# Adding two products in PSUM for the last four groups of a fused attention and rational-activation kernel, with the whole issue order written anew

## The chip, the cores and the metric

The kernel runs on one core of one Trainium2 chip. The metric is the device time of one execution in microseconds (us), lower is better. The core has five engines with in-order queues that run side by side: TensorE (PE in the profile, with its weight loads as PEld), VectorE (DVE), ScalarE (ACT), GpSimd (POOL) and SyncE (SP); sixteen DMA engines move data for all of them.

## The reference

Four batches, four heads, 1088 tokens and head dimension 32. Each head's queries and keys are turned into 64 features, the products of two projections; linear attention with these features gives `num / den`. The four heads side by side give 4352 tokens of 128 channels, and these go through one block with a rational activation:

```
phi(x)  = outer(S1 x, S2 x)                     # 8 x 8 = 64 features
x       = (phi(q) @ (phi(k)^T v)) / (phi(q) . sum phi(k) + 1e-6)
h       = x @ w_in                              # 128 -> 2048
P       = a0 + a1 h + a2 h^2 + a3 h^3
Q       = 1 + |b0| |h| + |b1| h^2
out     = (P / (Q + 1e-6)) @ w_out              # 2048 -> 128
```

The arrays are drawn from a fixed seed, and everything that comes in or goes out is float32.

## The kernel before, in words

The tokens are cut into ten chunks n: chunk 0 has 128 tokens, chunk 1 has 384, chunks 2 to 8 have 512 each, and chunk 9, the last, has 256 (64 left over from each batch). For each chunk the attention part (`add_keys`, `add_queries`) makes `xT`, 128 channels by the chunk's tokens. The 2048 hidden channels are 16 blocks of 128; a group g is one chunk with some of these blocks, laid side by side in the free dimension. There are 23 groups: 0 to 2 for chunk 0, 3 and 4 for chunk 1, two per chunk up to 18, and 19 to 22 for the last chunk, with 8, 4, 3 and 1 blocks (2048, 1024, 768 and 256 columns; `LAST`, line 159). A full group has 4096 columns.

`add_group` (from line 784) is one group. Its steps, by the names in the code:
- `h g,s`: TensorE multiplies by `w_in` in float32 into an `h_ps` tile of 1024 columns in PSUM. There are two such tiles, so `h` waits until the one before the last is emptied.
- `hev g,s`: the tile is cast to bf16 into `hb`. ScalarE does it; for the pieces in `CASTS` (line 161) VectorE does.
- `abs g` and `sq g`, VectorE: |h| into `u` (line 850) and h^2 into `lin` (line 858). The inputs are scaled at the start so that Q is 1 + kappa(|h| + h^2).
- `+Q g`: `u += lin`. With "Q" in the group's entry of `PLANS` (line 160) it is a DMA with an adding write that POOL issues (line 924), otherwise an addition on VectorE (line 920).
- `ln g` and `exp g`, ScalarE: ln(1 + kappa u) into `L` (line 872), and exp(-L), which is 1/Q, into `u` (line 875).
- `odd g`, `oddt g`, VectorE: the odd part of P into `y` (lines 862 and 868). `even g` (line 865) and `+P g` add the even part; `+P` goes by DMA with "P" in the plan.
- `n5 g`, VectorE: `y` times 1/Q (line 868).
- `py g`: TensorE multiplies `y` by the scaled `w_out` into `out_ps`. With "z" in the plan the constant a0 doesn't go through P: instead `pr g` multiplies `u` by a0 `w_out` into the same `out_ps`.
- `oev`, `otr`, `otev` and the store, per chunk: `out_ps` is copied by ScalarE, transposed by TensorE, copied again by ScalarE and stored by SP. They are numbered one less than the chunk: `oev 6` belongs to groups 15 and 16, `oev 7` to 17 and 18; for the last chunk there is only `otev 8`.
- `hot i`: a few bf16 matmuls of 512 columns on zeros into a spare tile, nothing uses them; `HOT` (line 164) gives their number.

The order of all this is not found when the kernel runs, nor by a scheduler: `Plan` collects the steps, and `ORDER` (line 19) is a written-out list of their numbers. `issue` emits them in this order, and each engine gets its own steps in this order. A step that has to wait holds up everything behind it on its engine. The costs and due times that stand in the `plan.add` calls are used only where there is no `ORDER`. The weights `w_out` are loaded by SP into a `y` tile; VectorE (`w0 0`, `w0 1`, line 436) and ScalarE (`w1 0`, `w1 1`, line 435) scale them once.

```
                nc.gpsimd.dma_start(out=dst(), in_=src(), accum_op=AX.add, max_dma_last_dim=GW)
...
        dq = add_up("+Q", u, sq, [ab, sp], g - 0.5)
        dq0 = dq if dq["engine"] == "DVE" else dq["after"][0]
        e = plan.add("ACT", gw * 0.846 + 170, ln, after=[dq, c_a] + got("L"), rank=g - 0.4, take=take("L"), name=f"ln {g}")
        e = used(plan.add("ACT", gw * 0.835 + 102, ex, after=[e], rank=g - 0.4, give=give("L"), name=f"exp {g}"), "L")
```

Of the kernel before, what the change touches and what calls it, by code (L numbers as in the profile page):

```python
# [16 lines left out]
PSUM = bass.MemoryType.PSUM  # L17

ORDER = [
# [36 lines left out]


class Plan:
# [66 lines left out]
def kernel(  # L125
# [31 lines left out]
    HEAD = 1  # L157
    FIRST = [4, 4, 8]
    LAST = [8, 4, 3, 1]
    PLANS = {**{g: "QP" for g in range(4, 20)}, **{g:"QPz" for g in range(13,20)},5:"QP",3:"Q",4:"sQP",17:"Qz",19:"QPz",20:"z",21:"z",22:"z"}  # L160
    CASTS = {18:(6,),16:(6,),14:(6,),12:(6,),17:(6,),13:(6,),15:(6,),11:(6,),10:(6,),8:(6,),9:(6,)}
    PACKED = (0, 9)
    BY_TOKEN = (9,)
    HOT = [6, 2, 5, 5, 6, 11, 4, 4, 6]
# [82 lines left out]
    def load(eng, fn, kb, n=1, rank=0.0, take=(), after=()):  # L247
        ring = landed[len(landed) + n - 9:][:1] if len(landed) + n > 8 else []
        i = plan.add(eng, (480 if eng == "SP" else 700) * n, lambda: fn(eng), after=list(after) + [last_of.get(eng)] + ring,
                     rank=rank, take=take, name="load")  # L250
        last_of[eng] = i
        if eng == "ACT":
            i = plan.add(eng, 1, lambda: None, after=[i], rank=rank, lag=1300, name="load")
        last_of["DMA"] = plan.add("DMA", kb * 1024 / 275, lambda: None, after=[i, last_of.get("DMA")], rank=rank,
                                  name="land")
        landed.extend([last_of["DMA"]] * n)
        return last_of["DMA"]
# [28 lines left out]
    ld["q", 0, 1] = load("SP", lambda e: load_main(e, "q_sb", q, 0, 1), 256, rank=-94)  # L286
    second = dict(mains(1))
    ld["wo"] = load("SP", load_wo, 800, rank=-93, take=["y"])
    ld["k", 1] = load("SP", second["k"], 512, 1, rank=-91, take=["kq"])
    ld["v", 1] = load("SP", second["v"], 512, NP, rank=-90, take=["v_aug"])  # L290
    ld["q", 1] = load("SP", second["q"], 512, 1, rank=-89, take=["kq"])
# [9 lines left out]

    zero = nc.const_aps.tensor(0.0, (128, 1), FP).bitcast(BF)[:, 0:1]
    ident = consts.tile([128, 128], FP, name="ident")
    mask4 = consts.tile([128, H], FP, name="mask4")
    mask12 = consts.tile([128, H, JC - HEAD], FP, name="mask12")
    mask2 = consts.tile([128, 2], FP, name="mask2")
# [80 lines left out]

    c_s12 = plan.add("DVE", 430, s_spread, after=[ld["s"], c_mask], rank=-98)
    c_s2 = plan.add("POOL", 250, s_expanded, after=[ld["s"], c_pool], rank=-3)
    c_m12 = plan.add("POOL", 100, pool_mask12, after=[c_pool], rank=-98.9, name="mask12")  # L390
    c_sw = {}
    for b in range(2):
# [391 lines left out]
    def add_group(g, G):  # L784
# [30 lines left out]
        def got(kind):  # L815
            return [T[kind, "got", n]] if packed else []
# [101 lines left out]
        def add_up(name, dst, src, after, rank, give=()):  # L918
            if name[1] not in how:
                return plan.add("DVE", tt, lambda: nc.vector.tensor_add(out=dst(), in0=dst(), in1=src()), after=after,  # L920
                                rank=rank, give=give, name=f"{name} {g}")

            def f():
                nc.gpsimd.dma_start(out=dst(), in_=src(), accum_op=AX.add, max_dma_last_dim=GW)  # L924
            p = plan.add("POOL", 1900, f, after=after, rank=rank, name=f"{name} {g}")
            return plan.add("DMA", -(-gw // 2048) * 2048 * 1.43 if gw > 1024 else gw * 1.43, lambda: None, after=[p], rank=rank, give=give, lag=900, name=f"{name} land {g}")
# [3 lines left out]
            sp = plan.add("ACT", gw * 0.835 + 102, square, after=hes + got("sq"), rank=g - 0.5, take=take("sq"), name=f"sq {g}")  # L930
        else:
            sp = plan.add("DVE", tt, square, after=hes + got("sq"), rank=g - 0.5, take=take("sq"), name=f"sq {g}")
        dq = add_up("+Q", u, sq, [ab, sp], g - 0.5)
        dq0 = dq if dq["engine"] == "DVE" else dq["after"][0]
        e = plan.add("ACT", gw * 0.846 + 170, ln, after=[dq, c_a] + got("L"), rank=g - 0.4, take=take("L"), name=f"ln {g}")
        e = used(plan.add("ACT", gw * 0.835 + 102, ex, after=[e], rank=g - 0.4, give=give("L"), name=f"exp {g}"), "L")
        p = plan.add("DVE", ts + 121, odd, after=[sp, c_a] + got("y"), rank=g - 0.3, take=take("y"), name=f"odd {g}")
        p = used(plan.add("DVE", tt, mul(y, y, ht), after=[p, ab], rank=g - 0.3, give=give("t"), name=f"oddt {g}"), "t")
# [146 lines left out]
```

## Time and profile before

| what | value |
|---|---|
| time, median of 3 runs (lowest to highest) | 246.72 us (246.26 to 246.79) |
| the profiled execution | 247.33 us |
| its span, first to last instruction | 245.3 us |
| busy: PE, DVE, ACT, POOL | 239.0, 223.5, 219.8, 48.4 us |

The profile is of one execution. The span leaves out 2.03 us around it. [...] Square brackets give the idle time before an instruction and who ended it.

### The profile page before, as it was taken

What the parts mean: (1) busy time and instruction counts of PE and PEld (TensorE: products, weight loads), DVE (VectorE), ACT (ScalarE), POOL (GpSimd) and SP (SyncE); (2) the same over time, 40 slices, a digit from 0 to 9 for tenths busy, and PEclk for the clock granted to TensorE, in tenths of its full rate; (3) what the DMA queues carried; (4) which work ended last, traced back from release to release, by engine and by line L of the source; (5) the groups of instructions that cost most, each with busy time, mean ns of one, the idle gap of its engine ahead of it and who ended that gap; (6) DMA issues with size and microseconds to landing.
All of it is one profiled execution on the core that took longest, in us unless ns stands there. A gap on an engine that the chain in (4) does not pass through costs nothing.

```text
span 245.3 us, 3066 instructions
## 1 busy us (share of the span) xinstructions
PE 239.0 (97%) x1148; PEld 138.4 (56%) x1148; DVE 223.5 (91%) x242; ACT 219.8 (90%) x199; POOL 48.4 (20%) x70
## 2 busy tenths in 40 slices
PE   8998999999999999999999999999999999999986
PEld 4887667665556486456464554435444444755453
DVE  0747889999999999999999999999999999999792
ACT  3237799898979998899999999999999999999993
POOL 7800021010121503011112111231311112111100
PEclk9999999999999999999999999999999999999999
DMA  6897706855869999999799999999999999999822
GB/s 159 266 319 178 259 12 123 165 169 97 150 117 184 174 191 222 212 196 179 128 181 180 184 175 176 229 170 187 184 187 191 212 191 172 193 194 188 158 88 64
DMA packets 22206, 42.96 MB, mean 175 GB/s; under 512 B 5536, under 2 KB 12720, under 8 KB 22064
## 3 DMA queue, kind: packets, MB, share of 16 engines
q0 software_dynamic: 8544, 31.74, 72.6%
q1 hardware_dynamic: 13360, 10.95, 14.6%
q8 instruction: 9, 0.15, 0.2%
q10 hardware_dynamic: 288, 0.08, 0.2%
q14 instruction: 5, 0.04, 0.0%
HBM read 8.82 MB, written 2.23 MB: 45 GB/s over the span
## 4 chain that ended last, share of the span: by engine, by line
PE 60%; ACT 35%; issue 3%; DVE 0%; ACTq 0%
PE h_ps L831 31%; ACT u L875 13%; ACT L L872 12%; PE w_ps L498 7%; ACT hb L838 6%; PE out_ps L888 4%; PE w_ps L463 3%; PE w_ps L627 3%; PE w_ps L685 2%; PE w_ps L673 2%; PE w_ps L617 2%; PE w_ps L454 1%; PE out_ps L359 1%; ACT q_pT L679 1%; ACT o_sb L893 1%
## 5 line engine op out<-in xcount | busy, mean ns | idle before, releaser
L831 PE MATMUL h_ps<-xT,w_in_sb 128*128 128x512 f32 (+3 forms) x320 | 126.3, 533 | 0.0
L831 PEld LDWEIGHTS h_ps<-xT,w_in_sb 128*128 128x128 f32 x320 | 55.5, 190 | 41.9 <-issue 31.9
L872 ACT ACTIVATE L<-u,kappa 128x4096 f32<-128x4096 bf16 (+6 forms) x23 | 66.2, 2884 | 0.1
L875 ACT ACTIVATE u<-L 128x4096 bf16<-128x4096 f32 (+6 forms) x23 | 64.3, 2801 | 0.1
L838 ACT CAST hb<-h_ps 128x1024 bf16<-128x1024 f32 (+3 forms) x53 | 54.5, 1051 | 4.8 <-PE h_ps L831 4.6
L924 POOL DMA_DIRECT2D u<-lin x17 | 20.8, 1224 | 120.4 <-DVE lin L858 29.0
L868 DVE TENSOR_TENSOR y<-y,u 128x4096 bf16<-128x4096 bf16 (+6 forms) x23 | 39.7, 1727 | 1.7 <-ACT u L875 1.6
L868 DVE TENSOR_TENSOR y<-y,hb 128x4096 bf16<-128x4096 bf16 (+6 forms) x23 | 39.5, 1725 | 0.0
L858 DVE TENSOR_TENSOR lin<-hb 128x4096 bf16<-128x4096 bf16 (+6 forms) x22 | 37.9, 1724 | 1.4 <-ACT hb L838 1.3
L888 PE MATMUL out_ps<-y,w_out_b 128*128 128x512 bf16 (+2 forms) x144 | 30.6, 355 | 0.2 <-DVE y L868 0.2
L924 POOL DMA_DIRECT2D y<-lin x15 | 19.0, 1268 | 59.5 <-DVE lin L865 27.0
L862 DVE TENSOR_SCALAR y<-lin,a_t 128x4096 bf16<-128x4096 bf16 (+6 forms) x23 | 24.6, 1068 | 0.3 <-ACT lin L856 0.2
L850 DVE TENSOR_SCALAR u<-hb 128x4096 int16<-128x4096 int16 (+6 forms) x23 | 21.6, 941 | 2.1 <-ACT hb L840 1.2
L888 PEld LDWEIGHTS <-w_out_b 128*128 128x128 bf16 x144 | 13.5, 98 | 16.0 <-issue 4.2
L498 PEld LDWEIGHTS w_ps<-v_aug,k_p 128*128 128x128 f32 x128 | 14.9, 192 | 1.4 <-ACT ab L470 0.8
L498 PE MATMUL w_ps<-v_aug,k_p 128*128 128x96 f32 x128 | 15.6, 276 | 0.0
L838 DVE CAST hb<-h_ps 128x1024 bf16<-128x1024 f32 x11 | 13.4, 1220 | 0.7 <-PE h_ps L831 0.7
L865 DVE TENSOR_SCALAR lin<-lin,a_t 128x4096 bf16<-128x4096 bf16 (+3 forms) x13 | 13.4, 1030 | 0.0
L673 PEld LDWEIGHTS w_ps<-ident,q_p 128*128 128x128 f32 x66 | 7.8, 141 | 7.5 <-issue 3.9
L1049 PE MATMUL w_ps<-const-float32-0.0 128*128 128x512 bf16 x49 | 11.8, 381 | 0.0
L679 ACT COPY q_pT<-w_ps 128x512 f32<-128x512 f32 (+2 forms) x18 | 10.9, 603 | 1.0 <-PE w_ps L673 1.0
L888 PE MATMUL out_ps<-u,w_out 128*128 128x512 bf16 x48 | 11.3, 379 | 0.0
(118 smaller groups left out, 226.6 us busy)
## 6 DMA issues: line engine op xcount, KB each, us to landing
u<-lin POOLq DMA_DIRECT2D x14, 1024.0 KB, 8.6
y<-lin POOLq DMA_DIRECT2D x13, 1024.0 KB, 9.5
v_aug<-in_v_dram SPq DMA_DIRECT2D x8, 256.0 KB, 4.9
out_dram<-oT SPq DMA_DIRECT2D x7, 256.0 KB, 7.5
kq<-in_k_dram SPq DMA_DIRECT2D x3, 512.0 KB, 4.7
kq<-in_q_dram SPq DMA_DIRECT2D x3, 512.0 KB, 7.7
u<-lin POOLq DMA_DIRECT2D x2, 768.0 KB, 7.0
w_in_sb<-in_moe_w_in_dram SPq DMA_DIRECT2D x1, 1024.0 KB, 6.6
```

The lines of the kernel that those rows point to most:

```text
L498: nc.tensor.matmul(kv_of((hp,))[:, 0], lhsT=lhs(hp), rhs=rhs(hp), start=(first and hp == hps[0]), stop=final, skip_group_check=True)
L831: nc.tensor.matmul(T["h", g, s][:, i * step:i * step + W], lhsT=w_in_sb[:, fi * 128:(fi + 1) * 128], rhs=T["xT", n][:, :W], start=True, st ...
L838: copy(out=T["t", g][:, s * W:(s + nsub) * W], in_=T["h", g, s][:, :nsub * W])
L850: nc.vector.tensor_scalar(out=u().bitcast(mybir.dt.int16), in0=ht().bitcast(mybir.dt.int16), scalar1=0x7FFF, scalar2=None, op0=AX.bitwise_and)
L858: nc.vector.tensor_mul(out=sq(), in0=ht(), in1=ht())
L862: nc.vector.tensor_scalar(out=y(), in0=sq(), scalar1=a_t[:, 3:4], scalar2=a_t[:, 1:2], op0=AX.mult, op1=AX.add)
L865: nc.vector.tensor_scalar(out=sq(), in0=sq(), scalar1=a_t[:, 0:1], scalar2=None, op0=AX.add)
L868: return lambda: nc.vector.tensor_mul(out=out(), in0=in0(), in1=in1())
L872: nc.scalar.activation(out=T["L", g][:, :gw], in_=u(), func=ACT.Ln, bias=1.0 + 1e-6, scale=kappa[:, 2:3])
L875: nc.scalar.activation(out=u(), in_=T["L", g][:, :gw], func=ACT.Exp, scale=-1.0)
L888: nc.tensor.matmul(T["o", n][:, :W], lhsT=w[:, fi, :], rhs=T[src, g][:, i * W:(i + 1) * W], start=(start and i == 0), stop=(stop and i == ...
L924: nc.gpsimd.dma_start(out=dst(), in_=src(), accum_op=AX.add, max_dma_last_dim=GW)
```

## The change

In groups 19 to 22 the sum |h| + h^2 isn't made in `u` any more, neither by DMA (group 19) nor by VectorE (20 to 22). A new step `qs g,c` has TensorE add up to 1024 columns at a time: for each 512 columns one matmul of a bf16 identity with `u` and one with `lin`, both into the same PSUM region, which is an `h_ps` tile. `ln` then reads PSUM. Group 19 has two such steps and two `ln` steps (`ln 19` and `ln 19,1`), the others one each. POOL makes the bf16 identity once at the start. The second cast of group 19 (`hev 19,4`) moves from ScalarE to VectorE. "P" stays by DMA in group 19, "z" stays in all four.

```
-    PLANS = {**{g: "QP" for g in range(4, 20)}, ...,17:"Qz",19:"QPz",20:"z",21:"z",22:"z"}
+    PLANS = {**{g: "QP" for g in range(4, 20)}, ...,17:"Qz",20:"ez",21:"ez",22:"ez",19:"ePz"}
-    CASTS = {18:(6,), ..., 8:(6,),9:(6,)}
+    CASTS = {18:(6,), ..., 9:(6,),8:(6,),19:(4,)}
...
+    ld["wo"] = plan.add("ST", 1, lambda: None, after=[ld["wo"]], rank=-93, lag=1200, name="w_out")
...
+    ident_b = consts.tile([128, 128], BF, name="ident_b")
...
+    c_ib = plan.add("POOL", 300, lambda: nc.gpsimd.tensor_copy(out=ident_b, in_=ident), after=[c_id, c_pool], rank=-1, name="ident_b")
...
+        def q_sum(c, w):
+            T["Q", g, c] = tile_of(hps, "h_ps", [128, 1024], FP)
+            for i in range(c, c + w, CW):
+                cols = slice(i, min(i + CW, c + w))
+                o = T["Q", g, c][:, i - c:cols.stop - c]
+                nc.tensor.matmul(o, lhsT=ident_b, rhs=u()[:, cols], start=True, stop=False)
+                nc.tensor.matmul(o, lhsT=ident_b, rhs=sq()[:, cols], start=False, stop=True)
+
+        def ln_of(c, w):
+            if c == 0:
+                new("L")
+            nc.scalar.activation(out=T["L", g][:, c:c + w], in_=T["Q", g, c][:, :w], func=ACT.Ln, bias=1.0 + 1e-6, scale=kappa[:, 2:3])
+
+        if "e" in how:
+            dq0 = ab
+            e = None
+            for c in range(0, gw, 1024):
+                w = min(1024, gw - c)
+                dq = plan.add("PE", 40 + w * 0.845, lambda c=c, w=w: q_sum(c, w), after=[ab, sp, c_ib], rank=g - 0.45, take=["h_ps"],
+                              name=f"qs {g},{c // 1024}")
+                e = plan.add("ACT", w * 0.846 + 170, lambda c=c, w=w: ln_of(c, w), after=[dq, c_a, e] + got("L"), rank=g - 0.4,
+                             take=take("L") if c == 0 else [], give=["h_ps"], name=f"ln {g}" + (f",{c // 1024}" if c else ""))
+        else:
```

The list `ORDER` is another one from its fourth number on, for the whole kernel and not for the last groups alone. Decoded into step names, these are the places that matter below (one engine each):

```
VectorE, start
before: zspread 0, zrem 0, w0 1, q dpr 0b, q dsum 0b, q dinv 0b, q scale 0b, q prod 0b, w0 0, abs 0, sq 2
after:  zspread 0, zrem 0, q dpr 0b, q dsum 0b, q dinv 0b, q scale 0b, q prod 0b, abs 1, q dpr 1, sq 2 ... abs 2, q dinv 1, w0 0 ... +P 2, w0 1
TensorE, start
before: q abc 0b, h 0,0, h 2,0, k tr (1,0), qp tr 0b,0, q abc 1, qp tr 0b,1, k tr (1,1), h 1,0, x mm 0b, k ab (1,0), h 3,0
after:  q abc 0b, h 1,0, h 2,0, k tr (1,0), q abc 1, qp tr 0b,0, h 0,0, qp tr 0b,1, k tr (1,1), k ab (1,0), x mm 0b, k ab (1,1), h 3,0
ScalarE, around group 7
before: ln 4, hev 6,4, hev 6,2, x ev 2, exp 4, qp ev 3,0, hev 7,0, k eva (2,0), hev 7,6, k ev (2,1), hev 7,2, qp ev 3,1, hev 7,4, ln 5
after:  ln 4, hev 7,0, qp ev 3,0, hev 7,2, exp 4, hev 7,6, hev 7,4, k ev (3,0), qp ev 3,1, k eva (2,0), hev 8,0, ln 5
ScalarE, end
before: ln 16, exp 16, hev 19,0, ln 17, hev 19,4, exp 17, hev 20,0, ln 18, oev 6, exp 18, otev 5, hev 21,0, ln 19, exp 19, oev 7, hev 22,0, ln 20, otev 6, exp 20, ln 21, exp 21, ln 22, exp 22, otev 7, otev 8
after:  ln 16, hev 22,0, exp 16, hev 19,0, hev 21,0, ln 17, hev 20,0, exp 17, oev 6, ln 18, exp 18, otev 5, ln 19, ln 19,1, exp 19, oev 7, ln 20, otev 6, exp 20, ln 21, exp 21, ln 22, otev 7, exp 22, otev 8
TensorE, end
before: py 15, otr 5, h 19,0, h 19,4, hot 2, hot 3, h 20,0, pr 16, py 16, h 21,0, hot 4, h 22,0, hot 5, pr 17, py 17, otr 6, pr 18, py 18, hot 6, otr 7, pr 19, py 19, pr 20 ... py 22, hot 7, hot 8
after:  h 22,0, py 15, h 21,0, h 19,0, otr 5, hot 3, h 20,0, h 19,4, hot 4, pr 16, py 16, hot 5, otr 6, pr 17, qs 19,1, qs 19,0, py 17, pr 18, qs 20,0, py 18, qs 21,0, otr 7, pr 19, qs 22,0, py 19, pr 20 ... py 22, hot 6, hot 7, hot 8
```

Before, `hot 0` and `hot 1` stand ahead of `py 15` as well; after, `hot 0`, `hot 1` and `hot 2` do. On POOL, `ident_b` stands ahead of the loads of `a` and `b`.

More of the change, by code (lines that the diff above doesn't have):

```diff
@@ L159 @@
     LAST = [8, 4, 3, 1]
-    PLANS = {**{g: "QP" for g in range(4, 20)}, **{g:"QPz" for g in range(13,20)},5:"QP",3:"Q",4:"sQP",17:"Qz",19:"QPz",20:"z",21:"z",22:"z"}
-    CASTS = {18:(6,),16:(6,),14:(6,),12:(6,),17:(6,),13:(6,),15:(6,),11:(6,),10:(6,),8:(6,),9:(6,)}
+    PLANS = {**{g: "QP" for g in range(4, 20)}, **{g:"QPz" for g in range(13,20)},5:"QP",3:"Q",4:"sQP",17:"Qz",20:"ez",21:"ez",22:"ez",19:"ePz"}
+    CASTS = {18:(6,),16:(6,),14:(6,),12:(6,),17:(6,),13:(6,),15:(6,),11:(6,),10:(6,),9:(6,),8:(6,),19:(4,)}
     PACKED = (0, 9)
@@ L932, in add_group @@
             sp = plan.add("DVE", tt, square, after=hes + got("sq"), rank=g - 0.5, take=take("sq"), name=f"sq {g}")
-        dq = add_up("+Q", u, sq, [ab, sp], g - 0.5)
-        dq0 = dq if dq["engine"] == "DVE" else dq["after"][0]
-        e = plan.add("ACT", gw * 0.846 + 170, ln, after=[dq, c_a] + got("L"), rank=g - 0.4, take=take("L"), name=f"ln {g}")
+        def q_sum(c, w):
[19 more added lines that the diff above has]
+        else:
+            dq = add_up("+Q", u, sq, [ab, sp], g - 0.5)
+            dq0 = dq if dq["engine"] == "DVE" else dq["after"][0]
+            e = plan.add("ACT", gw * 0.846 + 170, ln, after=[dq, c_a] + got("L"), rank=g - 0.4, take=take("L"), name=f"ln {g}")
         e = used(plan.add("ACT", gw * 0.835 + 102, ex, after=[e], rank=g - 0.4, give=give("L"), name=f"exp {g}"), "L")
```

72 rows, old and new, of the table ORDER are left out of this document.

## The prediction

> **What bounds the kernel now.** I read the page, then busy time by stretch, then the chain of waits, then the timelines of the engines where the chain changes hands.
>
> ```profile
> PE 60%; ACT 35%; issue 3%; DVE 0%; ACTq 0%
> ```
> ```profile
> 20.00:50.00 30.00, 29.26 (x160) 20.42 (x159) 26.38 (x47) 25.81 (x37) 2.44 (x2) 1.00 0.61 144
> 50.00:100.00 50.00, 50.00 (x238) 29.65 (x237) 49.64 (x38) 45.83 (x45) 10.28 (x8) 1.00 0.85 161
> 100.00:150.00 50.00, 50.00 (x212) 27.44 (x211) 49.47 (x43) 49.28 (x40) 9.42 (x8) 1.00 0.98 178
> 215.00:230.00 15.00, 14.79 (x70) 8.20 (x69) 13.74 (x12) 14.96 (x8) 2.94 (x3) 1.00 0.98 179
> 230.00:245.30 15.30, 12.20 (x103) 7.12 (x101) 10.48 (x20) 11.38 (x15) 0.00 (x1) 1.00 0.36 95
> ```
> ```profile
> 30.98 0.84 PE w_ps L463 x8
> ...
> 146.12 1.86 PE h_ps L831 x4
> ...
> 221.19 0.91 ACT hb L838
> ```
>
> The columns of the stretches are PE, PEld, DVE, ACT and POOL busy, then the granted clock and the DMA share. TensorE is busy without a gap from 50 to 150 and nearly so up to 230, VectorE for 99% of it, ScalarE for 92% up to 100 and all but wholly from 215 to 230. The chain is TensorE's up to 148 and ScalarE's afterwards: up to 148 the matmuls are late, after it ScalarE's queue is. But TensorE stays full after 148, too, since the fillers `hot` stand in its queue. So a microsecond saved counts only where all full engines save it, and one added to TensorE's queue counts as soon as something waits for the end of it.
>
> **The start.** In the list before, VectorE stands at the scaling of `w_out` until its load lands, ahead of the work on queries that TensorE waits for:
>
> ```profile
> 17.98 0.75 DVE L436 TENSOR_SCALAR w_out<-y,a_sb 128x1024 bf16<-128x1024 f32 x1 [2.27 <-DMA y<-in_moe_w_out_dram]
> ```
> ```profile
> 20.89 0.52 PE L673 MATMUL w_ps<-ident,q_p 128*128 128x128 f32 x3 [0.74 <-ACT kT L458]
> 156.34 1.09 PE L673 MATMUL w_ps<-ident,q_p 128*128 128x128 f32 x8 [0.46 <-DVE q_p L665]
> 213.24 2.35 PE L1049 MATMUL w_ps<-const-float32-0.0 128*128 128x512 bf16 x10
> 215.43 1.89 PE L831 MATMUL h_ps<-xT,w_in_sb 128*128 128x256 f32 x8
> 217.15 1.89 PE L888 MATMUL out_ps<-u,w_out 128*128 128x512 bf16 x8
> 219.25 1.89 PE L888 MATMUL out_ps<-y,w_out_b 128*128 128x512 bf16 x8 [0.21 <-DVE y L868]
> ```
>
> The new list puts both scalings behind the first groups' work, and puts `q abc 1`, whose operands are there, ahead of the transposes of q_p. So I take TensorE's wait of 0.74 at 20.9 as gone: 0 at worst, 1.0 at best (if the casts that now come earlier also let `k ab (1,1)` in ahead of `h 3,0`). Next in line there is ScalarE's copy of the keys at 20.2, so no more than that. That is the whole gain that TensorE can get at the front; it is busy from there to 148 and nothing in that stretch is taken out of it, only reordered. ScalarE gets it as well up to 148, since its idle time there is waiting for TensorE.
>
> The identity in bf16 costs POOL one copy ahead of the loads of a and b. A copy of 128x128 there took 0.31. VectorE came to b at 10.46 with no idle time before it, so its own products of keys and queries cover the load. I take nothing; if the load came only just in time, it would be 0.3 on VectorE.
>
> ```profile
> 6.28 0.31 POOL L380 COPY S2x<-SR 128x128 f32<-128x128 f32 x1
> ```
> ```profile
> 10.46 0.20 DVE L401 TENSOR_SCALAR b_pos<-b_sb 128x2 int32<-128x2 int32 x1
> ```
>
> **The end, ScalarE.** Its timeline from the last full group on:
>
> ```profile
> 220.79 1.30 ACT L838 CAST hb<-h_ps 128x1024 bf16<-128x1024 f32 x1
> 222.12 3.71 ACT L872 ACTIVATE L<-u,kappa 128x4096 f32<-128x4096 bf16 x1
> 225.74 0.57 ACT L893 COPY o_sb<-out_ps 128x512 f32<-128x512 f32 x1
> 226.21 3.62 ACT L875 ACTIVATE u<-L 128x4096 bf16<-128x4096 f32 x1
> 229.73 0.58 ACT L903 COPY oT<-w_ps 128x512 f32<-128x512 f32 x1
> 230.19 0.81 ACT L838 CAST hb<-h_ps 128x768 bf16<-128x768 f32 x1
> 230.88 2.03 ACT L872 ACTIVATE L<-u,kappa 128x2048 f32<-128x2048 bf16 x1
> 232.94 1.91 ACT L875 ACTIVATE u<-L 128x2048 bf16<-128x2048 f32 x1
> 234.76 0.57 ACT L893 COPY o_sb<-out_ps 128x512 f32<-128x512 f32 x1
> 235.22 0.38 ACT L838 CAST hb<-h_ps 128x256 bf16<-128x256 f32 x1
> 235.49 1.16 ACT L872 ACTIVATE L<-u,kappa 128x1024 f32<-128x1024 bf16 x1
> 236.54 0.58 ACT L903 COPY oT<-w_ps 128x512 f32<-128x512 f32 x1
> ...
> 240.53 0.57 ACT L903 COPY oT<-w_ps 128x512 f32<-128x512 f32 x1
> ```
>
> Prices are start to start. Behind `ln 18` the new list has less: `oev 6` goes ahead of it (225.74 to 226.21, 0.47), and so do the casts of groups 21 (0.69) and 22 (0.27). It has more: `otev 7`, which at 240.53 filled the wait for the last product, now stands ahead of the last exp (0.46), and two logarithms of 1024 columns at 1.05 replace one of 2048 at 2.06 (0.04; 0.2 if two fixed costs show fully, I take 0.1). A logarithm on PSUM isn't in this trace. The bounds are the casts on PSUM, 0.69 for 768 columns, as against some 0.8 for that many in a logarithm from SBUF: 0.1 less a piece, and as much more if it is dearer; I take the same, and plus or minus 0.5 over five pieces. Sum behind `ln 18`: 0.46 + 0.10 - 1.43 = -0.87.
>
> [...]
>
> Ahead of `ln 18` ScalarE gets the two casts and the copy (1.43) and loses the cast `hev 19,4` (0.9, as the cast at 221.19 in the chain): +0.5, which the start's gain covers.
>
> Of the DMA, group 18's sum landed just when it was wanted, 213.23 + 8.8 = 222.03 for `ln 18` at 222.12:
>
> ```profile
> 213.23 1.17 POOL L924 DMA_DIRECT2D u<-lin  x1 [8.72 <-ACT hb L838]
> ```
> ```profile
> u<-lin POOLq DMA_DIRECT2D x1, 1024.0 KB, 8.8
> ```
>
> VectorE's order up to that DMA's inputs changes by two passes' places, one product less ahead of them, so the sum should land no later. Group 19's DMA ended no wait: its logarithm at 230.88 followed ScalarE's cast without idle time. So taking it away wins nothing by itself. VectorE loses the additions of groups 20 to 22, 2048 columns together at the price of the second row below (its 0.68 for 1024, twice, 1.36 at most), and gains one cast of 1.21: even.
>
> ```profile
> 206.41 1.21 DVE L838 CAST hb<-h_ps 128x1024 bf16<-128x1024 f32 x1
> ...
> 232.07 0.68 DVE L920 TENSOR_TENSOR u<-u,lin 128x1024 bf16<-128x1024 bf16 x1
> ```
>
> **The end, TensorE.** This is the step I weigh most. `oev 6` now stands ahead of `ln 18`, and it waits for `py 16`. What is queued behind it is all of ScalarE's tail, and all of VectorE's `n5` behind that. Ahead of `py 16` the new list has more: `hot 4`, six matmuls at 0.219 (ten in 213.24 to 215.43), 1.31; the eight matmuls of groups 21 and 22 at 0.215 (eight in 215.43 to 217.15), 1.72. Together 3.03. It can win back its waits, 0.74, 0.46 and 0.21, and some tenths that lie between recorded ends and next starts: 1.4 to 2.0. Before, `py 16` ended at 219.25 + 1.73 = 220.98; after, at 222.0 to 222.6, say 222.3. With 0.1 for the hop (an estimate: half of the 0.21 idle at 219.25) and 0.47 for `oev 6`, `ln 18` starts at 222.9 in place of 222.12: +0.75. Without that wait ScalarE would come to it at 222.12 + 0.5 - 0.9 = 221.7.
>
> Further on TensorE has `hot 5` (11, 2.4), `otr 6` (four transposes, half of the eight at 156.34, 0.5), `pr 17`, `py 17`, `pr 18`, `py 18` (1.72 each), and three pieces of sums: 12 matmuls of 512 bf16 columns at 0.215, 2.6. So `py 18` ends at 222.3 + 12.3 = 234.6. ScalarE reaches `oev 7`, which waits for it, at 222.9 + 3.62 + 3.52 + 0.46 + 2.10 + 1.82 = 234.4: a wait of 0.3 with the hop. The sums themselves wait for nothing that is late: `qs 20,0` needs the tile that the first logarithm of group 19 gives back.
>
> **Sum** for the span: +0.75 at `ln 18`, -0.87 behind it, +0.3 at `oev 7`: +0.2, 245.5. The profiled execution lay 2.03 above its span and 0.61 above the median, so on the scale of the median 246.72 + 0.2 = 246.9.
>
> **The rivals.** *TensorE falls behind in the middle (slower).* The sum has TensorE without a wait from 25 to 222, and each one there is paid in full, the fillers being in its queue whatever happens. Place: two `h_ps` tiles, with the casts that free them behind a logarithm or an exp. In the new order around group 7, `hev 7,6` stands behind `exp 4` (3072 columns, three quarters of the 3.52 from 226.21 to 229.73 for 4096, 2.7), and TensorE has `h 7,4` and `k ab`, 1.72 + 0.84, before it needs that tile: a wait of 0.2 there; behind a full group's 3.5 it is 1.0. For: each full group has such a place, and the old list, with 50.00 busy of 50.00, shows none. Against: the new list spaces most of them by two products. It decides from 0.5 us in all; five or six places give 1.2: 248.0.
>
> *ScalarE alone sets the end (faster).* If TensorE wins more at the start or loses less than its sum, `ln 18` starts at 221.7, and the end is 0.4 + 0.9 earlier less the 0.1 to 0.3 that `oev 7` waits: -1.0, 245.7. For: before, `py 16` ended 4.7 us before `oev 6` at 225.74. Against: 3.03 is counted from rows.
>
> *The end doesn't move.* The tail's edits cancel and the start's wait comes back at the next place: 246.7.
>
> [...]
>
> **Numbers.** The forecast, 246.9 (246.4 to 247.4 with the pieces' 0.5), has 0.40; TensorE behind 0.33; ScalarE alone 0.20; no move 0.04; the clock 0.03. The range 245.7 to 248.3 takes in both large rivals with the doubt of the logarithm on one side and more waits on the other. A measurement of this kernel can tell 0.2%, 0.49 us, from no change, 246.23 to 247.21: of the forecast 0.28 lies inside, 0.02 below, 0.10 above. So faster 0.22, same 0.32, slower 0.46.
>
> **What would show it.** TensorE's wait at 20.9 gone and `h 3,0` no later; VectorE's 2.27 for `w_out` gone; `py 16` ending near 222.3 and ScalarE idle for about a microsecond ahead of `oev 6`, a little ahead of `oev 7`; a logarithm of 1024 from PSUM near 1.05. If TensorE shows waits between 50 and 200, the first rival holds. If ScalarE has no idle time before 241, the second does. A logarithm on PSUM that differs by 0.2 a piece would make the sum wrong.

## The result, and the profile after

The changed kernel takes 248.01 us (median of 5 runs, 247.83 to 248.92), the kernel before 246.79 in 5 runs beside it: 1.0051 times as long, 95% interval 1.0031 to 1.0071. It is 1.2 us slower, more than can be confused with no change. The profiled execution of after took 248.01 with a span of 246.3, that of before 247.33 with 245.3.

The chain that ended last, by engine, in after (before it was TensorE 60% and ScalarE 35%):

```profile
PE 39%; DVE 36%; DMA 9%; issue 7%; ACT 6%; SPq 3%; DVEq 0%
```

Now VectorE and the DMA are in it too: from 50 to 200 us VectorE is busy for 49.42 to 49.69 of each 50 us, ScalarE for 48.31 to 49.81, and the DMA share is 0.86 to 1.03, so which of them carries the chain says little. The stretches of after follow, in the columns that the prediction named (PE, PEld, DVE, ACT, POOL, clock, DMA share):

```profile
20.00:50.00 30.00, 29.32 (x171) 21.27 (x169) 25.91 (x46) 23.44 (x36) 2.25 (x2) 1.00 0.50 133
50.00:100.00 50.00, 50.00 (x233) 29.41 (x232) 49.57 (x40) 48.31 (x45) 11.43 (x9) 1.00 0.86 157
100.00:150.00 50.00, 50.00 (x210) 27.20 (x209) 49.69 (x42) 48.77 (x37) 10.38 (x9) 1.00 0.98 182
150.00:200.00 50.00, 49.86 (x180) 22.79 (x179) 49.42 (x36) 49.81 (x38) 9.40 (x8) 1.00 1.03 193
...
215.00:230.00 15.00, 15.00 (x73) 8.33 (x72) 14.88 (x12) 14.97 (x7) 1.18 (x1) 1.00 0.86 153
```

ScalarE does 2.4 less than before between 20 and 50 and 2.5 more between 50 and 100. The granted clock is 1.00 in every stretch of both profiles, so the clock, which has 0.03 among the chances, took no part. ScalarE's end in after follows (`oev 6` at 223.10, `ln 18` at 223.58, `oev 7` at 235.75, the last exp at 241.18). A row has the start in us from the span's start, then the recorded length. A record runs past the next start, here by some 0.1 (227.33 + 3.62 against 230.85), in before by up to 0.4 (217.27 + 3.92 against 220.79); why, no run shows. So a step's price on a busy engine is the distance from start to start:

```profile
205.64 3.71 ACT L875 ACTIVATE L<-u,kappa 128x4096 f32<-128x4096 bf16 x1
...
213.36 1.71 ACT L841 CAST hb<-h_ps 128x1024 bf16<-128x1024 f32 x2 [0.22 <-PE h_ps L834]
...
219.47 3.63 ACT L878 ACTIVATE u<-L 128x4096 bf16<-128x4096 f32 x1
223.10 0.59 ACT L896 COPY o_sb<-out_ps 128x512 f32<-128x512 f32 x1
223.58 3.71 ACT L875 ACTIVATE L<-u,kappa 128x4096 f32<-128x4096 bf16 x1
...
235.75 0.59 ACT L896 COPY o_sb<-out_ps 128x512 f32<-128x512 f32 x1 [0.36 <-PE out_ps L891]
236.23 1.12 ACT L948 ACTIVATE L<-h_ps,kappa 128x1024 f32<-128x1024 f32 x1
237.24 0.58 ACT L906 COPY oT<-w_ps 128x512 f32<-128x512 f32 x1
...
241.18 0.43 ACT L878 ACTIVATE u<-L 128x256 bf16<-128x256 f32 x1
```

`ln 18` starts 1.46 later than before (222.12). From it to the last exp's end after takes 18.04, before 18.51: 0.47 won, 0.57 was forecast. Behind the last exp both take 4.7. So 1.46 - 0.47 = 1.0 is the whole difference of the two profiled spans, and the question is why `ln 18` is late. ScalarE has no recorded idle time ahead of `oev 6` (from start to start it is 0.1 at most): it doesn't stand there for about a microsecond, waiting for TensorE, as the sum had it, but comes late itself. TensorE is late as well (`py 16` in the second row):

```profile
219.45 1.89 PE L891 MATMUL out_ps<-u,w_out 128*128 128x512 bf16 x8
221.17 1.89 PE L891 MATMUL out_ps<-y,w_out_b 128*128 128x512 bf16 x8
222.90 1.47 PE L1076 MATMUL w_ps<-const-float32-0.0 128*128 128x512 bf16 x6
```

`py 16` ends at 222.90, against 220.98 before and 222.3 in the forecast. At the start, VectorE's 2.27 at `w_out` is gone, and others stand in its place:

```profile
17.40 0.26 DVE L651 TENSOR_TENSOR den<-abc 128x96 f32<-128x96 f32 x1 [1.70 <-ACT abc L640]
...
22.52 0.30 DVE L651 TENSOR_TENSOR den<-abc 128x128 f32<-128x128 f32 x1 [2.26 <-ACT abc L640]
```

TensorE's 0.74 at 20.9 is gone too, and further on it has a wait that the old order didn't have, for ScalarE's copy `q ev 3` ahead of `x mm 1`:

```profile
44.20 1.08 PE L688 MATMUL w_ps<-q_pT,kv_bd 128*64 128x512 f32 x4 [0.68 <-ACT qT L624]
```

### The profile page after: what moved, and what is told of

Read it like the earlier page. It is cut to its first block, busy times and chain, and to the rows that moved or that the text cites. A ratio compares the mean times of both kernels' runs of the same rounds, so it can differ in the third digit from the quotient of the medians.

```text
span 246.3 us, 3098 instructions
## 1 busy us (share of the span) xinstructions
PE 241.6 (98%) x1166; PEld 140.2 (57%) x1166; DVE 224.0 (91%) x240; ACT 219.3 (89%) x199; POOL 48.6 (20%) x70
## 4 chain that ended last, share of the span: by engine, by line
PE 39%; DVE 36%; DMA 9%; issue 7%; ACT 6%; SPq 3%; DVEq 0%
PE h_ps L834 22%; DVE y L871 12%; DVE lin L861 8%; PE out_ps L891 6%; DMA kq<-in_k_dram 4%; DMA u<-lin 4%; DVE y L865 4%; DVE u L853 3%; DVE lin L868 2%; DVE hb L841 2%; ACT u L878 2%; DVE q_p L668 2%; PE w_ps L1076 2%; PE w_ps L688 2%; PE w_ps L501 2%
## 5 line engine op out<-in xcount | busy, mean ns | idle before, releaser
L878 ACT ACTIVATE u<-L 128x4096 bf16<-128x4096 f32 (+6 forms) x23 | 63.3, 2757 | 0.1
L875 ACT ACTIVATE L<-u,kappa 128x4096 f32<-128x4096 bf16 (+3 forms) x19 | 60.8, 3198 | 0.0
L841 ACT CAST hb<-h_ps 128x1024 bf16<-128x1024 f32 (+3 forms) x52 | 51.5, 1006 | 2.9 <-PE h_ps L834 2.6
L927 POOL DMA_DIRECT2D y<-lin x15 | 18.1, 1203 | 63.1 <-DVE lin L868 17.7
L841 DVE CAST hb<-h_ps 128x1024 bf16<-128x1024 f32 x12 | 14.5, 1212 | 0.6 <-PE h_ps L834 0.5
L484 DVE TENSOR_TENSOR k_p<-ab 128x1024 f32<-128x1024 f32 x8 | 9.7, 1226 | 1.7 <-ACT ab L473 1.7
```

The lines of the kernel that those rows point to most:

```text
L841: copy(out=T["t", g][:, s * W:(s + nsub) * W], in_=T["h", g, s][:, :nsub * W])
L875: nc.scalar.activation(out=T["L", g][:, :gw], in_=u(), func=ACT.Ln, bias=1.0 + 1e-6, scale=kappa[:, 2:3])
L878: nc.scalar.activation(out=u(), in_=T["L", g][:, :gw], func=ACT.Exp, scale=-1.0)
```

## The experiments

Each kernel was compared in five rounds with the kernel before on the same chip; the medians of before were 246.3 to 246.8. `ORDER` is given in step names.

### The start

`w0_late` changes one thing in the order of before:

```
 VectorE: ... zspread 0, zrem 0,
-w0 1, q dpr 0b, ... q prod 0b, w0 0, abs 0, sq 2 ... abs 2, q dinv 1, ...
+q dpr 0b, ... q prod 0b, abs 0, sq 2 ... abs 2, w0 0, w0 1, q dinv 1, ...
```

> The order of before, with only VectorE's two scalings of w_out moved from behind the first work on queries to behind the absolute value of group 2. If TensorE's wait of 0.74 at 20.9 hangs on that stall alone and comes back nowhere: 0.5 to 0.8 us faster than before, 246.0. If the gain is spent at the next wait (TensorE for ScalarE's copies, or VectorE for w_out's use): within 0.2 of before.

Measured: 246.33 against 246.53, ratio 0.9977 (0.9957 to 0.9997). The profiled execution has a span of 244.3, and every full group's logarithm and exp from 90 us (90.08 against 91.03) to 217 (216.33 against 217.27) starts 0.93 to 0.95 earlier than in the profile of before: a rigid shift, nothing in the middle takes it up or adds to it. But most executions of before come near that span too: the 69 beside these experiments have spans of 244.1 to 246.7, median 244.7. Only 12 have 245.2 or more, and the profiled one, with 245.3, is as long as those. The 12 executions of `w0_late` have 244.1 to 244.7, median 244.3. What differs shows in other kernels that have the old start. First the one with only the end new (`tail_new`, below):

```profile
18.51 0.75 DVE L439 TENSOR_SCALAR w_out<-y,a_sb 128x1024 bf16<-128x1024 f32 x1 [2.30 <-DMA y<-in_moe_w_out_dram]
```
```profile
21.42 0.52 PE L676 MATMUL w_ps<-ident,q_p 128*128 128x128 f32 x3 [0.72 <-ACT kT L461]
```

and then `nohot_old`, `late_seam` and `no_sum`:

```profile
16.76 0.75 DVE L436 TENSOR_SCALAR w_out<-y,a_sb 128x1024 bf16<-128x1024 f32 x1 [0.95 <-DMA y<-in_moe_w_out_dram]
```
```profile
16.89 0.75 DVE L439 TENSOR_SCALAR w_out<-y,a_sb 128x1024 bf16<-128x1024 f32 x1 [1.00 <-DMA y<-in_moe_w_out_dram]
```
```profile
16.81 0.75 DVE L436 TENSOR_SCALAR w_out<-y,a_sb 128x1024 bf16<-128x1024 f32 x1 [0.49 <-DMA y<-in_moe_w_out_dram]
```

In before and `tail_new`, where VectorE's wait for `w_out` ended at 17.98 and 18.51, TensorE waits 0.74 and 0.72 near 21; in these three, where it ended at 16.76 to 16.89, TensorE has no wait there. So the wait that the sum takes away at the start is one of the profiled execution and, by the spans, not of the usual one; the other long executions were not traced. The scalings moved alone win 0.2 in the median and 0.6 by the ratio, in which the long executions weigh, so the times leave open which case of the expectation holds.

`start_fix` (order of after) tries to take TensorE's new wait away:

```
-TensorE: q tr 3, q abc 2, x mm 1        ScalarE: q ev 3, q eva 2, x ev 1
+TensorE: x mm 1, q tr 3, q abc 2        ScalarE: x ev 1, q ev 3, q eva 2
```

> After, with TensorE's first product of the second block of queries (x mm 1) moved ahead of the transposes of the third block, and ScalarE's copy of it with it, so that its wait of 0.68 at 44.2 goes. If a delay at the start is carried to the end one for one: 0.3 to 0.6 faster than after. If it is absorbed in the middle: within 0.2 of after.

Measured: ratio 1.0083 (1.0065 to 1.0101), not faster than after. It tells little, since the wait only moved on:

```profile
45.36 1.13 PE L630 MATMUL w_ps<-W_abc,qT 128*128 128x96 f32 x8 [0.48 <-ACT qT L624]
```

The same copy of ScalarE is now waited for one product later; `ln 18` is 0.08 earlier than in after. What the 0.68 alone costs was not settled.

`start_new` is before's list with the new order up to `exp 6` on ScalarE, 92 us in:

> The list of before, but up to the sixth group's exp (some 92 us in) in the new order; the rest in the old order, no sums in PSUM. If the gain at the start lasts and the loss is all at the end (theory 1): 0.5 to 0.9 us faster than before, since the 0.74 that TensorE waited at 20.9 is gone and the end is the old one. If the start's gain is spent by the waits that the new order brings between 20 and 60 us (theory 2): within 0.2 of before, or slower by up to 0.5.

Measured: 248.83, ratio 1.0084 (1.0062 to 1.0105). Neither figure was met; the reason is the place where the two orders join:

```profile
98.30 1.98 PE L831 MATMUL h_ps<-xT,w_in_sb 128*128 128x512 f32 x4 [1.10 <-ACT hb L838]
101.39 1.98 PE L831 MATMUL h_ps<-xT,w_in_sb 128*128 128x512 f32 x4 [0.24 <-ACT hb L838]
```

1.34 of TensorE is lost there, since each order has put off other steps. Its `ln 16` (206.11) and `ln 18` (223.93) are both 1.8 later than in before. So this run doesn't price the start, but nothing between these two wins the delay back, as in `w0_late`.

### TensorE's queue

`fill_out` is after without the six matmuls of `hot 4`; `nohot_new` leaves out `hot 0` to `hot 4`; `nohot_old` is before without `hot 0` to `hot 3`:

```
-HOT = [6, 2, 5, 5, 6, 11, 4, 4, 6]
+HOT = [6, 2, 5, 5, 0, 11, 4, 4, 6]     fill_out (after)
+HOT = [0, 0, 0, 0, 0, 11, 4, 4, 6]     nohot_new (after)
+HOT = [0, 0, 0, 0, 6, 11, 4, 4, 6]     nohot_old (before)
```

> After, with the six fillers of hot 4 left out, which stand ahead of the product of group 16; no part of the computation is left out. Theory 1: that product ends up to 1.3 earlier, the logarithm of group 18 up to 1.1 earlier, and the time is 0.8 to 1.2 below that of after, 246.8 to 247.2. If VectorE or ScalarE, not TensorE's queue, is late at that product: 0 to 0.3 below after. If the clock falls without them: slower than after.

> After, with the fillers hot 0 to hot 4 left out (24 matmuls, some 5.2 us of TensorE, all ahead of the product of group 16); nothing of the computation is left out. Theory A (TensorE's queue is what ScalarE and VectorE wait for between 100 and 215, the fillers in it being paid in full): VectorE's waits of 0.21 and 0.27 and ScalarE's of 0.72, 0.35 and 0.22 for TensorE's tiles go at least in part, and the time is 0.4 to 1.0 below that of after. Theory B (the delay at the end is one carried from the start, all three engines are full): within 0.2 of after, and TensorE shows the waits instead.

> Before, with the fillers hot 0 to hot 3 left out (18 matmuls, some 3.9 us of TensorE). Control for the run without fillers of the new order: theory A: at most 0.2 faster than before, since in the old order only two waits of 0.2 on TensorE's tiles lie behind 110 us. Theory B: within 0.2 of before. Slower by over 0.3 would mean that the fillers keep something up.

Measured: 1.0059 (1.0040 to 1.0079), 1.0044 (1.0027 to 1.0061) and 1.0021 (0.9999 to 1.0044). The first two can't be told from after. The third is 0.5 slower than before by the ratio and 0.85 by the medians, though the interval just takes in no change: the case in which the fillers keep something up; half of its executions had a lower mean clock (0.993, last section), and the six at 1.00 have a median of 246.4, near the 246.26 of before. With 1.3 us less on TensorE `ln 18` starts 0.17 earlier (`oev 6` and `ln 18` of `fill_out`):

```profile
222.94 0.59 ACT L896 COPY o_sb<-out_ps 128x512 f32<-128x512 f32 x1
223.41 3.73 ACT L875 ACTIVATE L<-u,kappa 128x4096 f32<-128x4096 bf16 x1
```

and with 5.2 less (`nohot_new`) 0.03:

```profile
222.57 0.59 ACT L896 COPY o_sb<-out_ps 128x512 f32<-128x512 f32 x1
223.55 3.72 ACT L875 ACTIVATE L<-u,kappa 128x4096 f32<-128x4096 bf16 x1 [0.38 <-DMA u<-lin]
```
```profile
212.58 1.17 POOL L927 DMA_DIRECT2D u<-lin  x1 [7.20 <-DVE u L853]
```

Here ScalarE's waits for TensorE's tiles behind 150 us are gone, and `ln 18` then waits for the sum of group 18 by DMA, which lands at 223.5, 10.9 after its issue. In after it was issued at 212.99 and took 10.0 (the second line is the issue's size and its time to landing):

```profile
212.99 1.17 POOL L927 DMA_DIRECT2D u<-lin  x1 [7.54 <-DVE u L853]
```
```profile
u<-lin POOLq DMA_DIRECT2D x1, 1024.0 KB, 10.0
```

So it landed at 223.0, and TensorE (222.90), the DMA (223.0) and ScalarE (223.10, the start of `oev 6`) reach this point within 0.2 of each other: making one of them faster wins next to nothing. In the old order without fillers TensorE waits 2.33 for VectorE ahead of `py 16`:

```profile
218.32 1.89 PE L888 MATMUL out_ps<-y,w_out_b 128*128 128x512 bf16 x8 [2.33 <-DVE y L868]
```

So in the old list the fillers ahead of `py 16` filled time that TensorE had; TensorE's queue was not what this point waited for. The theory that its 3.03 us more set the delay alone falls: without them ScalarE and the DMA are as late. That in after TensorE by itself would have been late by about as much, at 222.90, these runs don't exclude.

### The end

`tail_new` has the old order up to `ln 12` on ScalarE (161 us), then the new one with the sums in PSUM; `late_seam` the old order up to `h 19,0` (205 us), then the new one; `end_old` is the complement of `late_seam`, new up to there, then the old end with the old sums.

> The list of after, but up to the twelfth group's logarithm (some 161 us in) in the old order; from there the new order with the sums in PSUM. Theory 1 (3.03 us more of matmuls stand ahead of the product of group 16 that the tail waits for; nothing wins them back but two waits of 0.46 and 0.21 and the slack that there was): 1.0 to 1.8 slower than before, about as after or more, with the logarithm of group 18 starting about 1.5 later than in before. Theory 2 (the loss lies ahead of 60 us): at most 0.5 slower than before. Theory 3 (the sums themselves cost little or win): behind that logarithm 0.4 to 0.6 less than before in either case.

> Before's order up to the first matmuls of group 19 (some 205 us in), then the new order with the sums in PSUM, hot 2 and 3 where the old list has them: the edit at the end by itself, on a start and a middle that are those of before. By the rows of the end (0.5 more on ScalarE ahead of the logarithm of group 18, 0.4 to 0.6 less behind it, a wait of 0.3 for the product of group 18): 0.1 to 0.5 slower than before if ScalarE's queue sets the end, 0.8 to 1.5 slower if TensorE's 3.03 us more ahead of the product of group 16 do. Theory of the start and the middle (the change's loss lies ahead of 205 us): under 0.5.

> The new order up to the first matmuls of group 19 (some 205 us in), then the old order's end, sums on VectorE and by DMA: the complement of the run with only the end new. Theory F (the front: the old order's start loses 0.74 on TensorE only in the executions in which the load of w_out lands late, as in the profiled one of before; in the others the new order has nothing to win there, keeps its own wait of 0.68 at 44.2 and then lets ScalarE wait 0.9 us more for TensorE's tiles between 100 and 215): 0.8 to 1.6 slower than before, like after; ScalarE's logarithm of group 18 at 222.6 to 223.2. Theory E (the loss is in the end: 0.5 more work on ScalarE ahead of that logarithm, 3.03 us more on TensorE): at most 0.4 slower than before, that logarithm at 222.1 or earlier.

Measured: `tail_new` 1.0079 (1.0056 to 1.0102), `late_seam` 1.0192 (1.0161 to 1.0222), `end_old` 1.0092 (1.0077 to 1.0107), that is 2.3, 5.4 and 2.2 us slower than before by the medians: all three lie above every range that was expected of them. In `tail_new`, `ln 18` starts 2.5 later than in before, and behind it the run takes 0.4 less, as theory 3 had it. In `late_seam` TensorE stands still ahead of `h 20,0`, and the whole end is late; TensorE's row, then ScalarE's:

```profile
214.39 3.72 PE L834 MATMUL h_ps<-xT,w_in_sb 128*128 128x256 f32 x16 [1.86 <-ACT hb L841]
```
```profile
209.55 0.37 ACT L841 CAST hb<-h_ps 128x256 bf16<-128x256 f32 x1 [1.68 <-PE h_ps L834]
...
225.10 0.59 ACT L896 COPY o_sb<-out_ps 128x512 f32<-128x512 f32 x1 [2.03 <-PE out_ps L891]
```

The sums take `h_ps` tiles, so `h 21,0` and `h 22,0` have to come ahead of group 19; `h 20,0` then waits for the tile of `h 21,0`, whose cast stands behind `exp 16`. In the new list the work up to 205 us is placed for this, in the old list it is not. The run prices that step on an order that isn't made for it, and not the end as after has it; `tail_new`, joined at 161 us, is 2.4 later than before at `ln 16` already (206.71 against 204.27). `end_old` joins better: there the two orders have done the same work but for one copy and a small product. It is slower than before though its end is the old one, so the loss lies in the first 205 us. By the ratios the new end wins some of it back. `ln 16` and `ln 18` of `end_old`:

```profile
205.87 3.71 ACT L872 ACTIVATE L<-u,kappa 128x4096 f32<-128x4096 bf16 x1
...
223.54 3.71 ACT L872 ACTIVATE L<-u,kappa 128x4096 f32<-128x4096 bf16 x1 [0.47 <-DMA u<-lin]
```

The same logarithm `ln 16` in `late_seam`, whose order up to there is the old one:

```profile
203.41 3.98 ACT L875 ACTIVATE L<-u,kappa 128x4096 f32<-128x4096 bf16 x1
```

At that point ScalarE has done the same work in all of them, but for the copy `otev 4` (0.46), which the new front has already done. So against the old order with an early load `end_old` is 2.0 late there and after (205.64) 1.8: this is the loss of the front, seen directly. ScalarE would have been at `ln 18` at 223.07, within the figures of the theory of the front, but waits 0.47 for the DMA and starts at 223.54, outside them.

That sum was issued at 214.58, 2.0 later than in `nohot_new`, and landed at the same time, 223.5. From issue to landing it took 8.8 in before and 8.9 in `end_old`, which have the old end, and 10.0 in after and 10.9 in `nohot_new`, which have the new one. Counted from the issue of the adding DMA before it, it landed after 18.7 in before (203.33 to 222.03) and in after (204.28 to 223.0), after 19.0 in `end_old` (204.51 to 223.5) and after 19.3 in `nohot_new` (204.21 to 223.5). The DMA share being 1.02 to 1.05 from 213 to 223 in before and after, the work that the DMA engines still had ahead of it may be the reason; no run tested that.

### What the sums are worth

`no_sum` leaves the sums of the last four groups out of before:

```
-        dq = add_up("+Q", u, sq, [ab, sp], g - 0.5)
+        dq = add_up("+Q", u, sq, [ab, sp], g - 0.5) if g < 19 else sp
...
-        e = plan.add("ACT", gw * 0.846 + 170, ln, after=[dq, c_a] + got("L"), ...
+        e = plan.add("ACT", gw * 0.846 + 170, ln, after=[dq, ab, c_a] + got("L"), ...
```

Its `ln` in these groups reads |h| alone, so its Q leaves out h^2 there.

`cast_dve` is `w0_late` with the casts of groups 21 and 22 on VectorE, ahead of `n5 18`; `sum_dve` adds to it the change's own edit for groups 20 to 22, with the bf16 identity on POOL:

```
-CASTS = {..., 9:(6,)}
+CASTS = {..., 9:(6,),21:(0,),22:(0,)}
-ScalarE: exp 18, otev 5, hev 21,0, ln 19, exp 19, oev 7, hev 22,0, ln 20
+ScalarE: exp 18, otev 5, ln 19, exp 19, oev 7, ln 20
-VectorE: oddt 19, n5 18
+VectorE: oddt 19, hev 21,0, hev 22,0, n5 18
 sum_dve, besides:
+PLANS = {..., 19:"QPz",20:"ez",21:"ez",22:"ez"}
+HOT = [6, 2, 5, 5, 6, 7, 4, 4, 6]
+TensorE: hot 5, pr 17, py 17, otr 6, qs 20,0, pr 18, py 18, qs 21,0, hot 6, otr 7, pr 19, py 19, qs 22,0, pr 20 ...
+VectorE: n5 18, sq 21, abs 21, oddt 20 ...
```

> Before, with the additions to the square left out in the last four groups (VectorE's three and one DMA); their logarithm reads the absolute value alone. The most that taking these sums off VectorE and the DMA could win. If VectorE has slack there (it waited 1.26 for the exp of group 18): 0 to 0.2 faster than before. If the additions are on the path: 0.7 to 1.4 faster.

> The order of before with w_out's scalings late, and the casts of groups 21 and 22 moved from ScalarE's end (0.69 and 0.27) to VectorE, into its wait of 1.26 ahead of the product of group 18; sums as in before. If ScalarE's queue behind the logarithm of group 18 sets the end: 0.6 to 0.9 faster than the run with only the scalings moved, 0.8 to 1.1 faster than before. If the sum of group 19 by DMA (landing near 230.0) or the product of group 18 takes ScalarE's place: 0 to 0.4.

> The run with the scalings late and the two casts on VectorE, and now the change's own edit in that place: the sums of groups 20, 21 and 22 by TensorE in PSUM (group 19's stays with the DMA), in stretches in which TensorE waited, hot 5 with 7 matmuls in place of 11. If VectorE's end, which let TensorE wait 1.20 for its last products in the run with the casts alone, is what kept that run from being faster, the three additions (0.68, 0.55 and 0.29, 1.5 us) off VectorE give 0.5 to 1.0 over that run: 0.6 to 1.2 faster than before, the span near 243.1. If TensorE's 1.7 us of sums stand ahead of the product of group 18 and make the copy behind it late, or the logarithm waits for them: within 0.3 of the run with the casts alone.

Measured: `no_sum` 1.0010 (0.9993 to 1.0027), `cast_dve` 0.9989 (0.9974 to 1.0003), `sum_dve` 0.9970 (0.9959 to 0.9982), 246.19 against 246.81. In the old list the sums cost nothing that these runs can measure, so moving them there can win next to nothing. With the casts gone ScalarE reached the last logarithm 1.05 earlier than in `w0_late`, but the span fell by 0.4 only, since VectorE now came last (TensorE's last products in `cast_dve`):

```profile
237.84 0.62 PE L883 MATMUL out_ps<-w_out_b,y 128*128 128x128 bf16 x8 [1.20 <-DVE y L868]
...
239.17 0.51 PE L883 MATMUL out_ps<-w_out_b,y 128*128 128x128 bf16 x6 [0.38 <-DVE y L868]
```

In `sum_dve`, with the change's edit in that place, both waits are gone, and from `ln 18` to the span's end it takes 22.83 against 23.06 in `cast_dve` and 23.3 in `w0_late`. The price is TensorE's time ahead of `py 18`, for which `oev 7` waits:

```profile
233.90 0.59 ACT L896 COPY o_sb<-out_ps 128x512 f32<-128x512 f32 x1 [0.59 <-PE out_ps L891]
```

`sum_dve` is faster than both kernels, by 0.3% (0.2 to 0.4) over before. How much of that the sums give isn't settled: its interval overlaps with that of `cast_dve`, over which it is 0.2% better, and with that of `w0_late` (0.9977), and its profiled span, 244.1, isn't shorter than the 243.9 of `cast_dve`; 243.1 was expected.

## Why the prediction was right or wrong

248.01 lies in the range, and slower was the likeliest sign, at 0.46. But the forecast was +0.2 and the result is +1.2, the figure of the first rival.

**The step that failed is the start**: "+0.5, which the start's gain covers". It took 0.74 to 1.0 from one wait of one execution. The times gave a hint: the profiled execution lay 0.61 above the median, and the sum carried that along as a constant. It was not one: against the three profiles with an early load and the same order, `ln 16` came 0.5 to 0.9 later in that execution. And it took the stretch from 25 to 200 as "only reordered", with its own rival on the other side. The idle time up to 200 us is read from the sum rows of the stretches (200 less the busy time), first of before, then of after, then of `late_seam`, which has the old order up to there and an early load:

```profile
sum 200.00, PE 197.07 PEld 114.47 DVE 184.45 ACT 178.42 POOL 41.95; mean PE 39.41 PEld 22.89 DVE 36.89 ACT 35.68 POOL 8.39
```
```profile
sum 200.00, PE 196.91 PEld 114.90 DVE 184.04 ACT 177.98 POOL 43.04; mean PE 39.38 PEld 22.98 DVE 36.81 ACT 35.60 POOL 8.61
```
```profile
sum 200.00, PE 198.06 PEld 115.35 DVE 185.35 ACT 179.29 POOL 42.05; mean PE 39.61 PEld 23.07 DVE 37.07 ACT 35.86 POOL 8.41
```

After has 1.31 more idle time on ScalarE than the old order with an early load, and 1.31 more on VectorE; against the profiled execution of before it is 0.44 and 0.41. In place of a gain of 0.7 to 1.0 there is a loss of 1.3 in idle time, of which the late load hid 0.9 in the profile of before. Of ScalarE's share 0.6 arises ahead of 100 us, about as much as TensorE's wait of 0.68 at 44.2, though no run took that wait out by itself, and 0.7 from 100 to 200, where its two longest waits are for TensorE's tiles:

```profile
139.34 0.59 ACT L624 COPY qT<-w_ps 128x512 f32<-128x512 f32 x1 [0.35 <-PE w_ps L630]
...
141.03 1.01 ACT L841 CAST hb<-h_ps 128x1024 bf16<-128x1024 f32 x1 [0.72 <-PE h_ps L834]
```

One reading ahead of the sum was loose, and nothing in the sum rests on it: VectorE's 99% doesn't hold from 215 to 230, where its row has 13.74 of 15.00. The other steps, in the order of the sum:
- *The identity on POOL costs nothing*: right, VectorE comes to `b` at 10.46 as before.
- *ScalarE's work ahead of `ln 18`, +0.5*: right. At `ln 16` ScalarE is 0.91 late against the profile of before (205.64 less 204.27, less the 0.46 of `otev 4`, which is already done); 0.91 + 0.5 makes the 1.46 within 0.05. That fits because two waits cancel which the sum doesn't have. In before a cast of 1024 columns ahead of a logarithm takes 0.89:

```profile
211.87 1.29 ACT L838 CAST hb<-h_ps 128x1024 bf16<-128x1024 f32 x1
212.76 4.01 ACT L872 ACTIVATE L<-u,kappa 128x4096 f32<-128x4096 bf16 x1
```

Ahead of `ln 18` it is 1.33 (220.79 to 222.12), so ScalarE waits some 0.44 there for the sum by DMA, a wait that the long record of the cast hides (1.30 for a price of 0.89): `ln 18` starts 0.1 behind the landing at 222.03. In `end_old` the wait shows, 0.47 ended by that DMA. In after ScalarE loses as much at 213.36 and ahead of `oev 6`. Of the 0.91, 0.44 is idle time; the rest is spread over many steps, and no run traced it to a cause.
- *Group 18's sum lands no later than 222.03*: wrong. It was issued 0.24 earlier than in before, but landed at 223.0, as it took 10.0 in place of 8.8. In after ScalarE comes to `ln 18` later still, so it costs nothing there; in `nohot_new` and `end_old` it landed at 223.5 and held `ln 18`.
- *TensorE's 3.03 set `oev 6`*: not the cause by itself, though its figure was near (222.90 for 222.3). `fill_out` and `nohot_new` took 1.3 and 5.2 of it away for nothing.
- *Behind `ln 18` -0.87, `oev 7` waits 0.3*: right, -0.47 together for -0.57, a wait of 0.36, and the logarithm of 1024 columns from PSUM costs 1.01 (236.23 to 237.24) where it cost 1.05 from SBUF (235.49 to 236.54). The two of group 19 take 2.16 (231.32 to 233.48) where the one of 2048 columns took 2.06 (230.88 to 232.94): the 0.10 of the sum. Without the wait, the part behind `ln 18` is -0.83, near the sum's -0.87.

**The rivals.** *TensorE falls behind in the middle* has the right time, by luck, and half of the mechanism: it is ScalarE and VectorE that wait for TensorE's tiles, at 139, 141, 197, 206 and 213, while TensorE itself has no wait over 0.15 from 45 to 230, and its price of five or six equal waits was not what happened. *ScalarE alone* was right in that ScalarE has no idle time to speak of ahead of `oev 6`, and wrong in the sign, for the reason of the start. Ahead of 205 us no step of the sums runs but the copy of the identity: what is slower is the rest of the new list, part of which may be placed for them. Which of its moves cost the time was not settled. Since no run has the new end on an old front without a loss at the joint, the end's own gain in after stays open: from `ln 16` to the end of the span after takes 40.66, `end_old` 40.83 and before 41.03, of which 0.46 is the copy that after has already done, so by the spans it is 0.2 at most, and by the ratios of after and `end_old` 1.0.

## What to carry to other kernels

Before a wait is priced as a gain, ask whether the usual execution has it: where the profiled execution is slower than the median, a wait of its trace may not be in the median, and a change that removes it then wins little. Here it was the wait for a load: 0.74 in the profiled execution, while `w0_late` won 0.2 in the median. In these kernels a delay at the start arrived at the end unchanged (before against `w0_late`: 0.95 at 90 us, 0.94 at 217), and taking fillers out won nothing that could be measured (`fill_out` 1.0059 and `nohot_new` 1.0044, after 1.0051). Where several engines reach a point within some tenths of each other, a run that relieves one of them can't tell whether it would have been late by itself. And an issue order rewritten as a whole has to be priced as a whole, by the idle time of each engine up to a point at which both orders have done the same work. Ask, too, whether the engine that work is taken off ends last: the sums were worth nothing measurable in the old list (`no_sum` 1.0010), and once VectorE had taken over two casts from ScalarE, moving three of them ended TensorE's wait of 1.20 for VectorE, though the gain in time, some 0.2%, isn't clear of noise.

## What the runs showed of the hardware

- The load of `w_out` took 8.6 to 8.9 from issue to landing in `nohot_old`, `late_seam`, `nohot_new` and `w0_late`, and 9.8 to 10.3 in before, after and `tail_new`. In the four profiles with the old order up to `ln 16`, that logarithm came at 203.33 (`nohot_old`), 203.41 (`late_seam`) and 203.82 (`no_sum`), where VectorE's wait for the load ended before 17, and at 204.27 in before, where it ended at 17.98.
- Group 18's sum, 1 MB by DMA, took 8.8 to 10.9 from issue to landing in before, after, `end_old` and `nohot_new`, at a DMA share of 1.02 to 1.05 (before and after, 213 to 223); issued at 212.58 (`nohot_new`) and at 214.58 (`end_old`) it landed at 223.5 in both. So here a duration from issue to landing, taken from another order, was no price.
- Without the fillers of the old order (`nohot_old`) six of twelve executions had a mean granted clock of 0.993 in place of 1.00, and took 247.0 to 248.5 against 246.1 to 247.2 for the six others; in `late_seam`, where TensorE stands still for 1.86, four of six did, in `end_old` two of four and in `cast_dve` one of eleven; in `nohot_new`, without 24 fillers of the new order, none of seven did. The profiled executions were at 1.00, so where in the run the clock fell, and behind what, was not seen.
